# Gated scan and mixture of experts: softmax sums travel with the rows, running offsets are copied sooner, two selections go to GpSimd, and one unit's transposes move ahead of its rank matmuls

## The chip, the cores and the metric

One core of a Trainium2 chip runs the whole program. The metric is the device time of one execution in microseconds, shown as the median of several runs. A core has TensorE (PE; its loading of weights is PEld), VectorE (DVE), ScalarE (ACT), GpSimd (POOL) and SyncE (SP), each with its own queue, and 16 DMA engines that all queues share.

## The reference

```python
# x, f_logit: [4, 3648, 256]; lower_bound: [256]; all float32
sig = 1 / (1 + exp(-f_logit))
f = lower_bound + (1 - lower_bound) * sig
for t in range(3648):                       # per sequence
    h = f[:, t] * h + (1 - f[:, t]) * x[:, t];  y[:, t] = h
x = y.reshape(14592, 256)
g_logits = x @ w_group                      # [N, 4]
g_idx = argmax(g_logits);  g_sm = exp(g_logits - max)
g_w = (g_sm / (sum(g_sm) + 1e-9))[g_idx]
for g in range(4):                          # rows with g_idx == g
    e_logits = xg @ w_expert[g]             # [., 4]; e_idx, e_w in the same way
    for e in range(4):                      # rows with e_idx == e
        h = relu(xg @ w1[g, e])             # [., 1024]
        out[tok] = g_w * e_w * (h @ w2[g, e])
```

Sixteen experts, 14592 tokens of 256 values, a hidden width of 1024. Since the chosen logit is the greatest, its exponential is 1, and the weight of a row is one over the product of two softmax sums.

## The kernel before, in words

**Phase 1** goes through the tokens in 29 units of 512 (`UNIT`; the last has 256), with the 256 channels in two halves on the partitions. Per unit: load x and the gate logits (`p1_load`), tanh and an affine pass on ScalarE (`p1_tanh`, `p1_affine`), the gate's product and two scans on VectorE (`p1_tb`, `p1_gate`, lines 250, 261, 271), router logits on TensorE (`p1_router`, `p1_logits`, lines 308, 321), and `p1_back`, which transposes h on TensorE (line 289) and copies it with ScalarE into `rows` (line 291), a tile of 512 rows by `RW` = 258 words: 256 values, the token's number (line 293) and its weight.

**Routing** works on a group of units (`GROUPS`: eight single units, ten pairs, a last single one); `route_thunks` cuts it into steps. `s1` and `s2` find maxima and the one-hot of the winner on VectorE, `f3` the one-hot over 16 experts, `f4` the rank matmuls on TensorE (lines 423 to 426), which add up ranks and the running offsets of the 16 lists, `f4x` the exponentials on ScalarE, `s6` the sums (four VectorE operations, lines 367 to 374), `f5` the position of each row (lines 437, 439) and the copy of the new running offset to SBUF (`runoff`, line 441, ScalarE), `s8` the reciprocal into the last column of `rows` (line 380), `s7` the scatters: one indirect DMA by GpSimd for 128 rows into the list of their expert, `xs` (line 398). Later groups use `s3`, `s4`, `s5` instead of `f3`, `f4`, `f5`. `choose` and `place` read the running offset: `choose` picks the fullest lists that were not yet picked, `place` says which rows of a list may be read already.

**Phase 2** multiplies. Sixteen early jobs of kind A take 256 to 640 rows of a picked list each as soon as phase 1 has passed a cut (`EARLY`), while phase 1 goes on; sixteen late jobs of kind B take what is left, in an order that `order` computes when all is routed. Rows come back from `xs` by `job_rows`; the weight and the number travel with them, in `xr` and `meta` for A, in `info` and `joint` for B. `job_xt` transposes and splits a float32 number into two 16-bit parts, `job_split` does so for weights (lines 995, 997), `m1_step` multiplies by w1, takes the relu on ScalarE and the rest of the split on VectorE (lines 1133 to 1139), `m2_step` multiplies by w2 (line 1165), scales with ScalarE by the row's weight (line 1177) and scatters to the output (line 1179). The first four jobs (`RAW`) use float32 throughout (lines 1102, 1146). A chunk's `m2_step` calls come behind the `m1_step` calls of the chunk that follows, in the first four jobs right behind its own.

**Order.** `p1_thunks` lists phase 1 as small steps; `bg_step` mixes them into the jobs at a rate that due times set. `back(u - 1)` in that list puts the transposes of a unit in two steps; for units from 6 on they stand in front of `s1` already, before that behind `f4`. The start, until unit 5's routing, is in order as written for PE, DVE and ACT; later on a planner orders these engines within the limits that the program sets. SP's queue is in the order of the program.

Of the kernel before, what the change touches and what calls it, by code (L numbers as in the profile page):

```python
# [56 lines left out]
def gated_scan_moe(ctx: ExitStack, tc, zx, lower, wroute, wexp, out, S):  # L57
# [12 lines left out]
    RW = D + 2  # L70
# [70 lines left out]
    dmat = iota_f32("dmat", [P], [[1, P]], mult=-1)  # L141
# [186 lines left out]
    def route_thunks(G, T, fast=False):  # L328
# [3 lines left out]
        def s1():  # L332
# [3 lines left out]
            ge = R["ge"] = rt.tile([P, T, 5, 4], F32, name="ge")  # L336
            V.tensor_tensor(out=ge, in0=lg, in1=mx[:, :, :, None].broadcast_to([P, T, 5, 4]), op=ALU.subtract)

        def s2():
# [4 lines left out]
            oh = R["oh"] = rt.tile([P, T, 5, 4], F32, name="oh")  # L344
# [563 lines left out]
    def job_rows(j):  # L908
# [528 lines left out]
```

## Time and profile before

| | us |
|---|---|
| median of 3 runs | 746.05 (746.03 to 747.53) |
| profiled execution | 747.26 |
| its span, first to last instruction | 745.2 |
| TensorE busy | 707.5 (95%) |
| VectorE busy | 513.8 (69%) |
| ScalarE busy | 444.9 (60%) |
| GpSimd busy | 302.6 (41%) |
| mean granted clock of TensorE | 0.992 of full speed |

The profile is of one execution. Busy time counts an engine's own instructions; a matmul's end is modelled. In a timeline, a bracket behind an instruction holds how long its engine idled in front of it and what released it. Lines are those of the program printed above. The chain that ended last lies for 63% of the span on TensorE and for 13% on VectorE.

### The profile page before, as it was taken

How to read it: one execution, taken by the hardware profiler on the slowest of the kernel's cores; microseconds unless marked ns; L12 is line 12 of the kernel's file. 1: busy time of each engine (PE TensorE's matmuls, PEld its weight loads, DVE VectorE, ACT ScalarE, POOL GpSimd, SP SyncE). 2: the span in 40 equal slices, each digit the busy share in tenths (PEclk: the TensorE clock that was granted, in tenths of full speed). 3: DMA queues.
4: the chain of work that ended last, by engine and by line, in shares of the span. 5: the costliest groups of instructions: out<-in, count | busy, mean ns of one | idle time of the engine just before them, and what ended most of it. 6: DMA issues, size and time to landing. Idle time of an engine off the chain costs nothing.

```text
span 745.2 us, 18005 instructions
## 1 busy us (share of the span) xinstructions
PE 707.5 (95%) x6539; PEld 582.4 (78%) x6543; DVE 513.8 (69%) x1084; ACT 444.9 (60%) x824; POOL 302.6 (41%) x330
## 2 busy tenths in 40 slices
PE   2669999999999999999999999999999999999996
PEld 1457888888888888889989676877698888767795
DVE  6989658899999966595655755467336665676630
ACT  6667767986787864554555644566346555565531
POOL 3767367668877864632212111221131311212222
PEclk9989999999999999999999999999999999999998
DMA  8988799989999872747993281753362674666100
GB/s 326 414 293 280 238 371 288 413 295 315 322 327 288 242 233 71 221 108 199 209 223 111 91 188 38 180 154 117 114 163 99 193 193 150 181 186 189 41 30 31
DMA packets 99787, 151.36 MB, mean 203 GB/s; under 512 B 59593, under 2 KB 69594, under 8 KB 96880
## 3 DMA queue, kind: packets, MB, share of 16 engines
q1 hardware_dynamic: 85408, 102.83, 47.4%
q0 software_dynamic: 11168, 30.02, 10.8%
q10 hardware_dynamic: 3120, 17.34, 6.7%
q8 instruction: 52, 0.85, 0.5%
q14 instruction: 39, 0.32, 0.1%
HBM read 112.48 MB, written 37.93 MB: 202 GB/s over the span
## 4 chain that ended last, share of the span: by engine, by line
PE 63%; DVE 13%; issue 12%; DMA 4%; ACT 3%; POOL 3%; SPq 1%; POOLq 0%; DVEq 0%; ACTq 0%
PE ps_m L1165 25%; PE ps_m L1133 6%; PE ps_m L1135 6%; PE ps_m L1134 6%; PE ps_m L1146 4%; PE ps_m L1102 4%; DVE h L261 3%; POOL out_dram L1179 3%; PE ps_p L1135 3%; PE ps_p L1133 2%; PE ps_p L289 2%; PE ps_p L1134 2%; DVE w L997 2%; DMA xs<-rows,posi 2%; DVE hl L1139 2%
## 5 line engine op out<-in xcount | busy, mean ns | idle before, releaser
L1165 PE MATMUL ps_m<-w,hh 128*128 128x256 f16 (+4 forms) x1140 | 208.9, 272 | 0.0
L1165 PE MATMUL ps_m<-w,hl 128*128 128x256 f16 (+4 forms) x676 | 180.0, 271 | 0.0
L997 DVE TENSOR_TENSOR w<-st,w 128x1024 bf16<-128x1024 f32 x112 | 135.6, 1219 | 53.5 <-ACT w L995 52.0
L398 POOL DMA_INDIRECT xs<-rows,posi x114 | 136.5, 1198 | 73.8 <-ACT rows L293 20.7
L1179 POOL DMA_INDIRECT out_dram<-o,info x61 | 64.2, 1053 | 234.3 <-ACT o L1177 198.9
L1165 PE MATMUL ps_m<-w,rows 128*128 128x256 f16 (+4 forms) x848 | 128.4, 267 | 0.0
L995 ACT CAST w<-st 128x1024 f16<-128x1024 f32 x112 | 116.0, 1045 | 15.6 <-PE ps_m L1165 11.2
L1133 PE MATMUL ps_m<-xh,w 128*128 128x256 f16 (+9 forms) x494 | 120.4, 257 | 2.4 <-DVE hl L1139 2.4
L1165 PEld LDWEIGHTS <-hh 128*128 128x128 f16 (+5 forms) x1140 | 111.3, 100 | 12.4
L1135 PE MATMUL ps_m<-xh,w 128*128 128x256 f16 (+9 forms) x494 | 120.3, 257 | 0.0
L1134 PE MATMUL ps_m<-xl,w 128*128 128x256 bf16 (+9 forms) x494 | 120.3, 257 | 0.0
L1139 DVE SCALAR_TENSOR_TENSOR hl<-ps_m,hh 128x512 bf16<-128x512 f32 (+7 forms) x107 | 71.5, 672 | 45.5 <-ACT hh L1138 45.5
L1134 PEld LDWEIGHTS <-w 128*128 128x128 f16 x800 | 78.2, 98 | 24.8 <-issue 3.0
L1133 PEld LDWEIGHTS <-w 128*128 128x128 f16 x800 | 78.2, 98 | 23.4 <-issue 1.8
L1179 POOL DMA_INDIRECT out_dram<-o,meta x47 | 54.3, 1155 | 103.6 <-ACT o L1177 82.2
L1135 PEld LDWEIGHTS <-w 128*128 128x128 bf16 x800 | 78.1, 98 | 22.7 <-issue 0.2
L1165 PEld LDWEIGHTS <-rows 128*128 128x128 f16 (+3 forms) x848 | 77.9, 100 | 10.0 <-issue 0.6
L1138 ACT ACTIVATE hh<-ps_m 128x512 f16<-128x512 f32 (+7 forms) x107 | 63.3, 592 | 34.6 <-PE ps_m L1135 33.4
L1177 ACT ACTIVATE o<-ps_m,info 128x256 f32<-128x256 f32 (+6 forms) x61 | 28.5, 468 | 82.2 <-PE ps_m L1165 65.3
L1165 PEld LDWEIGHTS <-hl 128*128 128x128 bf16 (+4 forms) x676 | 66.2, 100 | 6.9
L261 DVE TENSOR_TENSOR_SCAN h<-zt,h 128x512 f32<-128x512 f32 (+3 forms) x48 | 56.8, 1194 | 2.0 <-PE ps_p L289 1.5
L1138 ACT ACTIVATE rows<-ps_p 128x512 f16<-128x512 f32 (+7 forms) x60 | 31.0, 516 | 24.8 <-PE ps_p L1135 24.7
(209 smaller groups left out, 1211.6 us busy)
## 6 DMA issues: line engine op xcount, KB each, us to landing
st<-in_wexp_dram SPq DMA_DIRECT2D x112, 512.0 KB
zt<-in_zx_dram ACTq DMA_DIRECT2D x16, 1024.0 KB
w<-in_wexp_dram SPq DMA_DIRECT2D x16, 512.0 KB
xs<-blank SPq DMA_DIRECT2D x26, 258.0 KB
zt<-in_zx_dram SPq DMA_DIRECT2D x6, 1024.0 KB
st<-in_zx_dram SPq DMA_DIRECT2D x8, 512.0 KB
xr<-xs SPq DMA_DIRECT2D x12, 258.0 KB
xr<-xs SPq DMA_DIRECT2D x16, 129.0 KB
```

Source lines behind the costliest of these rows:

```text
L261: sn = nc.vector.tensor_tensor_scan(out=h[:, k, c0 - a:c1 - a], data0=ff[:, k, c0 - a:c1 - a], data1=uu[:, k, c0 - a:c1 - a], initial=init ...
L398: sc = nc.gpsimd.indirect_dma_start(out=xs_v[G["t0"] + t][:, :], out_offset=bass.IndirectOffsetOnAxis(ap=R["posi"][:, t:t + 1], axis=0), i ...
L995: nc.scalar.copy(j.wh[i], j.st[i])
L997: nc.vector.tensor_tensor(out=j.wl[i], in0=j.st[i], in1=j.wh[i], op=ALU.subtract)
L1102: nc.tensor.matmul(pm[:, n * w:(n + 1) * w], (j.wh, j.wl)[c // 4][k][:, c % 4 * P:(c % 4 + 1) * P], x[:, 0:w], start=(k == 0), stop=(k == ...
L1133: nc.tensor.matmul(po, w1_at(j.wh, k, c), xh[:, k], start=(k == 0), stop=False)
L1134: nc.tensor.matmul(po, w1_at(j.wh, k, c), xl[:, k], start=False, stop=False)
L1135: nc.tensor.matmul(po, w1_at(j.wl, k, c), xh[:, k], start=False, stop=(k == KD - 1))
L1138: eviction[0] = nc.scalar.activation(hi, pv, AF.Relu).ins
L1139: nc.vector.scalar_tensor_tensor(out=h_at(j.hl[ch], cs, slice(0, w)), in0=pv, scalar=0.0, in1=hi, op0=ALU.max, op1=ALU.subtract)
L1165: nc.tensor.matmul(pm[i * q:i * q + n, 0:dw], h_at(h[ch], [c], ts)[:, 0], w2_at(w, c)[:, i * dw:(i + 1) * dw], start=(c == 0 and s == 0), ...
L1179: nc.gpsimd.indirect_dma_start(out=out_v[out_n[0]].rearrange("n (g d) -> (n g) d", g=g), out_offset=bass.IndirectOffsetOnAxis(ap=lt[s, r, ...
```

## The change

Five things are done. (1) A row has 262 words instead of 258: `s6` writes the five sums, four of them masked by the winning group, straight into `rows`, two VectorE operations for each unit of a group, and `s8` with the reciprocal is gone. The product and the reciprocal are made by `shares`, three VectorE operations, called behind the last `m1_step` of a chunk (kind A) or of a job's first chunk (kind B), and the scaling reads its result `wt`. All that carries the metadata is six words wide instead of two. (2) The copy of the running offset is a step of its own, `f5r`; in units up to `FAST` it stands in front of `back`. (3) Where `choose` picks two jobs with different cuts, their selections run on GpSimd. (4) `back` of unit 3 stands in front of `s1`. (5) `ge` and `oh` have one buffer, and `dmat` borrows the tile `rs`.

```diff
-    RW = D + 2
+    RW = D + 6
+    nc.gpsimd.memset(blank.bitcast(F32)[:, D + 1:RW], 1.0)
-    dmat = iota_f32("dmat", [P], [[1, P]], mult=-1)
+    dmat = p1.tile([P, P], F32, name="rs")
+    nc.gpsimd.iota(dmat, pattern=[[1, P]], base=0, channel_multiplier=-1, ...)
...
         def s6():
-            sm = rt.tile([P, T, 5], F32, name="sm", bufs=1)
-            V.tensor_reduce(out=sm, in_=R["ex"], axis=AX, op=ALU.add)
-            se = rt.tile([P, T, 4], F32, name="se", bufs=1)
-            V.scalar_tensor_tensor(out=se, in0=sm[:, :, 1:5], scalar=1e-9, in1=R["oh"][:, :, 0, :],
-                                   op0=ALU.add, op1=ALU.mult)
-            s1_ = rt.tile([P, T], F32, name="s1")
-            V.tensor_reduce(out=s1_, in_=se, axis=AX, op=ALU.add)
-            s2_ = rt.tile([P, T], F32, name="s2")
-            V.scalar_tensor_tensor(out=s2_, in0=sm[:, :, 0], scalar=1e-9, in1=s1_, op0=ALU.add, op1=ALU.mult)
-            R["s2"] = s2_
-
-        def s8():
             at = 0
             for rows, n in G["rows"]:
-                V.reciprocal(rows[:, 0:n, D + 1], R["s2"][:, at:at + n])
+                sm = rows[:, 0:n, D + 1:RW]
+                V.tensor_reduce(out=sm, in_=R["ex"][:, at:at + n], axis=AX, op=ALU.add)
+                V.scalar_tensor_tensor(out=sm[:, :, 1:5], in0=sm[:, :, 1:5], scalar=1e-9, in1=R["oh"][:, at:at + n, 0, :],
+                                       op0=ALU.add, op1=ALU.mult)
                 at += n
...
             placed[G["t0"]] = V.tensor_reduce(out=posi, in_=sc, axis=AX, op=ALU.add).ins
+            if not R.get("run"):
+                f5r()
+
+        def f5r():
+            pv = R["pp"][:, 0:(T + 1) * NE].rearrange("p (t e) -> p t e", e=NE)
             new = state["runoff"] = rt.tile([P, NE], F32, name="runoff")
             nc.scalar.copy(new, pv[:, T])
+            R["run"] = True
...
                     put(lambda u=u: p1_tanh(u + 1))
+                    if u == EARLY[0][0]:
+                        back(u - 1)
                     put(s1)
...
                     put(lambda u=u: p1_affine(u + 1))
+                    put(f5.soon)
                     back(u - 1)
...
+        B = nc.gpsimd if u >= BOOK else V
...
-                V.tensor_scalar(out=one, in0=key, scalar1=top[:, k:k + 1], scalar2=None, op0=ALU.is_equal)
+                B.tensor_scalar(out=one, in0=key, scalar1=top[:, k:k + 1], scalar2=None, op0=ALU.is_equal)
...
+    def shares(meta, n):
+        v = meta.bitcast(F32)
+        both = mo.tile([P, MT + 1], F32, name="both", bufs=2)
+        nc.vector.tensor_reduce(out=both[:, 0:n], in_=v[:, 0:n, 2:6], axis=AX, op=ALU.add)
+        nc.vector.scalar_tensor_tensor(out=both[:, 0:n], in0=v[:, 0:n, 1], scalar=1e-9, in1=both[:, 0:n],
+                                       op0=ALU.add, op1=ALU.mult)
+        wt = mo.tile([P, MT + 1], F32, name="wt", bufs=6)
+        nc.vector.reciprocal(wt[:, 0:n], both[:, 0:n])
+        return wt
+
+    def job_shares(j, ch):
+        if j.kind == "B":
+            n = sum(len(p) for p in j.parts)
+            if ch == 0 and n:
+                j.wt[0] = shares(j.info, n)
+            if ch == 0 and j.idx in SECOND:
+                j.wt["joint"] = shares(j.joint, 1)
+            return
+        a, w = j.chunks[ch]
+        for pi, (b, n) in enumerate(j.pieces):
+            if a <= b < a + w:
+                j.wt[pi] = shares(j.meta[pi], n // P)
...
+        if cs[-1] == KF - 1:
+            job_shares(j, ch)
...
-        nc.scalar.activation(o[s, 0:dw], pm[s, 0:dw], AF.Copy, scale=lt.bitcast(F32)[s, r, 1:2])
+        nc.scalar.activation(o[s, 0:dw], pm[s, 0:dw], AF.Copy, scale=wt[s, r:r + 1])
```

## Rows read from the trace of the kernel before

**Rows 1.** Windows: stretch, length, busy us by engine (instructions), clock, DMA share, GB/s
```profile
0.00:60.40 60.40, 34.06 (x276) 25.23 (x277) 49.20 (x152) 39.66 (x82) 36.66 (x66) 0.94 0.92 350
60.40:132.70 72.30, 72.30 (x500) 60.70 (x500) 53.15 (x123) 50.73 (x110) 44.63 (x56) 1.00 0.86 291
132.70:255.50 122.80, 119.79 (x1249) 104.28 (x1248) 121.51 (x243) 101.61 (x192) 92.58 (x86) 1.00 0.93 315
255.50:745.20 489.70, 481.32 (x4517) 392.19 (x4520) 289.91 (x568) 252.89 (x444) 128.74 (x125) 1.00 0.52 144
```

**Rows 2.** Timeline of TensorE: start, length, line, tiles, in brackets the idle before
```profile
51.65 0.21 PE L424 MATMUL ps_p<-oh16f,upto 128*128 128x64 bf16 x1 [3.19 <-DVE oh16f L412]
...
60.38 0.19 PE L424 MATMUL ps_p<-oh16f,upto 128*128 128x64 bf16 x1 [0.75 <-DVE oh16f L412]
...
159.48 0.27 PE L1133 MATMUL ps_m<-xh,w 128*128 128x256 f16 x1 [1.09 <-DVE hl L1139]
...
256.20 0.27 PE L1133 MATMUL ps_m<-xh,w 128*128 128x256 f16 x1 [0.99 <-DVE hl L1139]
...
328.58 0.27 PE L1133 MATMUL ps_m<-xh,w 128*128 128x256 f16 x1 [0.33 <-DVE hl L1139]
```

**Rows 3.** Timeline of VectorE, the end of unit 2's routing
```profile
28.70 0.17 DVE L369 SCALAR_TENSOR_TENSOR se<-sm,oh 128x16 f32<-128x16 f32 x1
28.91 0.17 DVE L372 TENSOR_REDUCE s<-se 128x4 f32<-128x16 f32 x1
...
29.20 0.22 DVE L437 TENSOR_TENSOR sc<-ps_p,oh16f 128x64 f32<-128x64 f32 x1
...
29.59 0.17 DVE L380 RECIPROCAL rows<-s 128x4 f32<-128x4 f32 x1
29.67 1.25 DVE L261 TENSOR_TENSOR_SCAN h<-zt,h 128x512 f32<-128x512 f32 x1
```

**Rows 4.** Timeline of TensorE, rank matmuls and transposes of units 2 and 3
```profile
28.60 0.32 PE L426 MATMUL ps_p<-oh16f,ones 128*128 128x64 bf16 x4
28.77 1.95 PE L289 MATMUL ps_p<-ident,h 128*128 128x128 f32 x8
...
36.17 0.21 PE L424 MATMUL ps_p<-oh16f,upto 128*128 128x64 bf16 x1 [2.83 <-DVE oh16f L412]
```

**Rows 5.** Timeline of ScalarE, units 2 and 3
```profile
27.71 1.50 ACT L234 ACTIVATE st<-st,mid,half 128x512 f32<-128x512 f32 x2
...
30.75 0.59 ACT L291 COPY rows<-ps_p 128x512 f32<-128x512 f32 x1 [0.17 <-PE ps_p L289]
31.24 0.18 ACT L441 COPY runoff<-ps_p 128x16 f32<-128x16 f32 x1
...
35.12 0.27 ACT L432 ACTIVATE ex<-ge 128x80 f32<-128x80 f32 x1 [1.21 <-DVE ge L337]
```

**Rows 6.** Timeline of VectorE, readers of the running offset, and two selections
```profile
31.52 0.18 DVE L660 SCALAR_TENSOR_TENSOR fill<-runoff,least 128x16 f32<-128x16 f32 x1 [0.59 <-ACT runoff L441]
...
39.04 0.18 DVE L706 SCALAR_TENSOR_TENSOR posA<-runoff,taken 128x16 int32<-128x16 f32 x1 [0.53 <-ACT runoff L441]
...
39.93 0.35 DVE L674 TENSOR_SCALAR sel<-fill,top 128x16 f32<-128x16 f32 x2
```

**Rows 7.** Timeline of GpSimd: a selection, first scatters of units 3 and 4
```profile
37.52 1.01 POOL L683 TENSOR_TENSOR least<-least,gone 128x16 f32<-128x16 f32 x1
38.69 1.05 POOL L398 DMA_INDIRECT xs<-rows,posi  x1 [0.16 <-DVE h L261]
...
46.46 1.05 POOL L398 DMA_INDIRECT xs<-rows,posi  x1 [1.60 <-ACT rows L293]
```

**Rows 8.** Timeline of SyncE's queue: the first expert rows
```profile
47.48 0.89 SPq L970 DMA_DIRECT2D xr<-xs  x2
```

**Rows 9.** VectorE by line and form, 132.7 to 255.5: count, busy us, mean ns, idle
```profile
L1139 DVE SCALAR_TENSOR_TENSOR hl<-ps_m,hh 128x512 bf16<-128x512 f32 x37 | 24.7, 677 | 0.2 <-ACT hh L1138 0.2
...
L367 DVE TENSOR_REDUCE sm<-ex 128x40 f32<-128x160 f32 x5 | 1.5, 308 | 0.0
```

More of the change, by code (lines that the diff above doesn't have):

```diff
@@ L140, in gated_scan_moe @@
     nc.gpsimd.memset(nowhere, N)
[L141 removed]
+    dmat = p1.tile([P, P], F32, name="rs")
+    nc.gpsimd.iota(dmat, pattern=[[1, P]], base=0, channel_multiplier=-1, allow_small_or_imprecise_dtypes=True)
     tri = const.tile([P, P], BF16, name="tri")
@@ L335, in s1 @@
             V.tensor_reduce(out=mx, in_=lg, axis=AX, op=ALU.max)
-            ge = R["ge"] = rt.tile([P, T, 5, 4], F32, name="ge")
+            ge = R["ge"] = rt.tile([P, T, 5, 4], F32, name="ge", bufs=1)
             V.tensor_tensor(out=ge, in0=lg, in1=mx[:, :, :, None].broadcast_to([P, T, 5, 4]), op=ALU.subtract)
@@ L343, in s2 @@
             V.tensor_reduce(out=pm, in_=pw, axis=AX, op=ALU.max)
-            oh = R["oh"] = rt.tile([P, T, 5, 4], F32, name="oh")
+            oh = R["oh"] = rt.tile([P, T, 5, 4], F32, name="oh", bufs=1)
             V.tensor_tensor(out=oh, in0=pw, in1=pm[:, :, :, None].broadcast_to([P, T, 5, 4]), op=ALU.is_equal)
@@ L447, in route_thunks @@
         if fast:
-            return s1, f4x, s2, f3, f4, s6, lambda: (f5(), s8()), s7s
-        return s1, s2, s3, s4, s5, lambda: (s6(), s8()), s7s
+            f5.soon = f5r
+            return s1, f4x, s2, f3, f4, s6, f5, s7s
+        return s1, s2, s3, s4, s5, s6, s7s
     def p1_thunks(us, groups, parts):
@@ L886, in make_job @@
         j.xh, j.xl = {}, {}
+        j.wt = {}
         return j
@@ L929, in job_rows @@
                     in_=xs[bass.ds(pos, j.blocks * 32), q * KD * 32:(q + 1) * KD * 32].rearrange("(i p) c -> p i c", p=32))
-            j.info = mo.tile([P, MT + 1, 2], I32, name="info", bufs=6)
+            j.info = mo.tile([P, MT + 1, RW - D], I32, name="info", bufs=6)
             if j.side:
@@ L933, in job_rows @@
                 if j.idx in PAIRS:
-                    joint[j.idx] = mo.tile([P, 2], I32, name="joint", bufs=2)
+                    joint[j.idx] = mo.tile([P, 1, RW - D], I32, name="joint", bufs=2)
                 j.joint = joint[SECOND.get(j.idx, j.idx)]
-                sync.dma_start(out=j.joint[at:at + n], in_=xs[bass.ds(pos + b, n), D:D + 2])
+                sync.dma_start(out=j.joint[at:at + n, 0], in_=xs[bass.ds(pos + b, n), D:RW])
             full = [p for ps_ in j.parts for p in ps_ if p[2] == 1]
@@ L963, in job_rows @@
                         early_loads.append(ld.ins)
-                    meta = mo.tile([P, 2, 2], I32, name="meta", bufs=16)
+                    meta = mo.tile([P, 2, RW - D], I32, name="meta", bufs=16)
                     ld = queue.dma_start(out=meta[:, 0:m],
-                                         in_=xs[bass.ds(at, w), D:D + 2].rearrange("(t p) c -> p t c", p=P))
+                                         in_=xs[bass.ds(at, w), D:RW].rearrange("(t p) c -> p t c", p=P))
                     early_loads.append(ld.ins)
@@ L1025, in job_xt @@
                                             scalar2=float(at - b), op0=ALU.subtract, op1=ALU.is_ge)
-                    nc.vector.copy_predicated(out=j.joint[s, 0:1], mask=gone[s], data=nowhere[s, 0:1])
+                    nc.vector.copy_predicated(out=j.joint[s, 0, 0:1], mask=gone[s], data=nowhere[s, 0:1])
                 if nf:
@@ L1075, in job_xt @@
         if j.raw:
-            j.meta.append(r[:, 0:m, D:D + 2])
+            j.meta.append(r[:, 0:m, D:RW])
             return
-        meta = mo.tile([P, 2, 2], I32, name="meta", bufs=16)
-        tc.keep_in_program_order(nc.vector.tensor_copy(meta[:, 0:m], r[:, 0:m, D:D + 2]))
+        meta = mo.tile([P, 2, RW - D], I32, name="meta", bufs=16)
+        tc.keep_in_program_order(nc.vector.tensor_copy(meta[:, 0:m], r[:, 0:m, D:RW]))
         if j.kind != "A":
@@ L1140, in m1_step @@
                                        op0=ALU.max, op1=ALU.subtract)
+        if cs[-1] == KF - 1:
+            job_shares(j, ch)
     def raw2(j, ch, t, cs, pm):
@@ L1169, in m2_step @@
         if j.kind == "B":
-            lt, r = j.info, b // P
+            lt, wt, r = j.info, j.wt[0], b // P
             if g > 1:
@@ L1203, in m2_joint @@
         o = mo.tile([P, D], F32, name="o", bufs=O_BUFS)
-        nc.scalar.activation(o, pm[:, 0:D], AF.Copy, scale=b.joint.bitcast(F32)[:, 1:2])
-        nc.gpsimd.indirect_dma_start(out=out_v[out_n[0]], out_offset=bass.IndirectOffsetOnAxis(ap=b.joint[:, 0:1], axis=0),
+        nc.scalar.activation(o, pm[:, 0:D], AF.Copy, scale=b.wt["joint"][:, 0:1])
+        nc.gpsimd.indirect_dma_start(out=out_v[out_n[0]], out_offset=bass.IndirectOffsetOnAxis(ap=b.joint[:, 0, 0:1], axis=0),
                                      in_=o, in_offset=None, bounds_check=N - 1, oob_is_err=False)
```

7 lines of the change are left out of this document (3 added, 4 removed).

## Prediction

> **What bounds the kernel now.** I read the windows first, cut where the limit changes [rows 1]. Up to 60.4 us TensorE works 34.06 of 60.40 us, so 26.3 of its 37.7 idle us lie in the start. From 60.4 to 132.7 it is busy 72.30 of 72.30: nothing but its own work counts. From 132.7 to 255.5 VectorE is busy 121.51 of 122.80 us and TensorE 119.79: two engines at their limit, and the 3.0 us that TensorE loses are there. Behind 255.5 TensorE is busy 481.32 of 489.70 us, most of the rest being the last eviction and scatter, and VectorE only 289.91.
>
> The timeline of TensorE says who holds it [rows 2]. The rank matmuls of units 5 and 6 (51.65, 60.38) wait 3.19 and 0.75 us for VectorE's one-hot. Later it has three waits of about 1 us, the first 1.09 at 159.48, the last 0.99 at 256.20, all for VectorE, and one of 0.33 at 328.58. So the sum has two sides: what VectorE saves ahead of 60 us moves everything forward, and what it is given between 132.7 and 255.5 comes back as stalls.
>
> **The change, part by part.**
>
> *Softmax sums, at the start.* Today, behind the gate's product (28.70), two more small operations follow at a pitch of 0.21 (28.70 to 28.91, operations that depend on each other), then the position product at 29.20, the reciprocal at 29.59, the next scan at 29.67, 0.08 behind it (operations that don't depend) [rows 3]. Without the two, the position product could start at 28.70 + 0.08 = 28.78, but its input, the rank matmuls, ends at 28.60 + 0.32 = 28.92 [rows 4]; I take 28.97. That gains 0.23, and the reciprocal's 0.08 goes too: 0.31 a unit. Five units (0 to 4) stand ahead of the rank matmuls of unit 5, in a row in which VectorE hardly waits: 1.55 us. Bounds: 5 x 0.08 = 0.4 (only the reciprocal) and 5 x 0.58 = 2.9 (two dependent steps and two independent ones).
>
> *Offsets copied sooner.* The copy of the running offset runs at 31.24, behind two copies of rows (the second 30.75, 0.59 long) [rows 5], and VectorE waits 0.59 us for it at 31.52 and 0.53 at 39.04 [rows 6]. Behind the affine pass it can start at 27.71 + 1.50 = 29.21, where the rank matmuls are done (28.92) [rows 4, 5]; VectorE asks only after its scan (29.67 + about 1.25). Both waits go: 1.12 us. What is late next there is nothing on the list; VectorE goes straight on to the gate. Behind the copy on ScalarE stand the row copies, held by their transposes anyway; cost 0, and 0.18 a unit without that cover. From unit 10 on the copy stays where it was.
>
> *Selections.* Two on VectorE at 39.93 took 0.35, some 0.26 of the chain [rows 6]. On GpSimd they stand in front of unit 4's scatters, where it idles 1.60 us until 46.46 [rows 7]. Gain 0.26; cost 0, and at worst 2 x 1.01 (the longest small GpSimd operation, at 37.52, ran 1.01 [rows 7]) less the 1.60, so 0.4 on a scatter.
>
> *Transposes of unit 3 ahead of its rank matmuls.* Eight take 1.95 us (28.77) and fall into a gap of 2.83 us in front of 36.17 [rows 4]. ScalarE's two copies of 0.59 and a short one go ahead of the exponential at 35.12, in front of which it idles 1.21 [rows 5]: it may come 0.2 late, and the sum that needs it stands five operations further on. Value 0; from -0.5 (if unit 3's scatters start sooner after all) to +0.2. No DMA is issued in another order; its scatters gain little: GpSimd is busy with the selection until 37.52 + 1.01 = 38.53 and begins unit 3 at 38.69 [rows 7].
>
> Sum to 51.65: 1.55 + 1.12 + 0.26 = 2.9. From 51.65 to 60.38 TensorE idles only the 0.75 [rows 2], and unit 5 gives VectorE its saving of 0.31 and a shorter wait there, so I add 0.7: **3.6 us gained at 60.4**, bounds 1.5 and 4.9. The first expert's rows are no brake: their load is issued at 47.48 [rows 8], and the transposes need it behind the rank matmuls and eight transposes, at 51.65 - 2.9 + 1.95 = 50.7.
>
> *Shares downstream, 60.4 to 132.7.* Four jobs add three small VectorE operations each; VectorE has 72.30 - 53.15 = 19 us free [rows 1]. Cost 0, at most 4 x 0.51 = 2.0 without that.
>
> *Shares downstream, 132.7 to 255.5.* In this stretch 37 evictions of 512 columns run on VectorE [rows 9]; at four for a chunk of 256 rows and two for one of 128, that is six jobs with ten chunks (4+4, 6+6, 8+8 evictions; the 37th begins the next). So ten calls, thirty operations of about 0.17 (reciprocal 29.59, reduction 28.91 [rows 3]). One call costs 3 x 0.09 = 0.27 if other work stands between its steps, and 0.21 + 0.21 + 0.09 = 0.51 if not; I take 0.39, the middle, since the order of VectorE here is a planner's and both kinds of neighbour occur: 3.9 us. Five routing groups go from six operations to four [rows 9]; the wide reduction of 0.31 becomes two of 0.23, so that a group saves 0.2 at the shorter pitch and nothing at the longer: 1.0 us. VectorE has 1.29 us unused [rows 1]; I let 0.6 soak up. The bill: 3.9 - 1.0 - 0.6 = **2.3 us**, bounds 0.4 (2.7 - 1.0 - 1.3) and 5.1 (ten by 0.51). As VectorE's queue is full from end to end, it reaches TensorE at 256.20 whole.
>
> In the rows dependent neighbours follow at 0.21 and independent ones at 0.08, though one takes 0.17 [rows 3]. The Trainium skill, "VectorE: DVE Perf Modes", Rules for kernel authors, tells instead to minimize the count of operations, because a drain follows each whatever it depends on. By it the net twenty operations cost 20 x 0.17 = 3.4 us (an estimate) and the sum becomes -3.6 + 3.4 - 0.6 + 0.4 = -0.4; the trace agrees with it for dependent neighbours only.
>
> *Behind 255.5.* Each of the 16 late jobs and three joint tiles gets a call (19 x 0.51 = 9.7 us if it were all on the path), but VectorE has 200 us free there and the tile that reads the share is evicted a chunk later: 0. At 328.58, where VectorE is late already by 0.33 [rows 2], one call more in front costs 0.4 (bounds 0 and 0.5). Rows longer by 16 of 1032 bytes: 1.6% on scatters and row loads, up to 60.4 us beside DMA engines at 0.92, on no wait above; 0, at most 0.3. Smaller buffers for routing tiles make VectorE wait for VectorE only: 0.
>
> **Sum.** -3.6 + 2.3 + 0.4 = -0.9 us. On the profiled execution (747.26, span 745.20 and 2.06 around it) that gives 746.4; the median shown is 746.05, 1.21 lower, so the prediction is 746.05 - 0.9 = 745.15, own range 743.8 to 746.5 (a bill of 0.9 to 3.7).
>
> **Rivals.**
> 1. *The bill is hidden.* Planned anew, the calls lie where VectorE would wait, or where its lateness doesn't reach TensorE. For: in 122.80 us of full VectorE TensorE has only three long waits [rows 2], so there is play between the two. Against: VectorE has 1.29 us unused in 122.80. Bill 0.4, no late stall: -3.2, 742.85.
> 2. *The bill outgrows the gain.* One mechanism: the three steps of a call stand next to each other behind the last eviction of a chunk, 0.51 each, nothing is saved in the groups, none soaks up, and the start gives only 2.9 (unit 6 still waits): -2.9 + 5.1 + 0.4 = +2.6, 748.65. It decides from a bill above the gain of the start, so above 0.3 us a call when the start gives 2.9. For: dependent steps at full pitch in [rows 3]. Against: in the full stretch there is always other work to stand between.
> 3. *The start is held by the first rows, not by VectorE.* GpSimd's scatters are back to back (38.53, 38.69) and move only by three units' saving, 3 x 0.31 = 0.9, and if loading the rows takes over, the gain is 0.9: -0.9 + 2.3 + 0.4 = +1.8, 747.85. Against: 47.48 is 3.2 us ahead of the need.
> 4. *Every operation costs its full length.* VectorE's 20 net operations by 0.17, less 0.6 of unused time: -0.4, 745.65. Against: the pitch of 0.08 [rows 3]. (This is the count rule of the Trainium skill, "VectorE: DVE Perf Modes", named above.)
>
> **Chances.** Forecast 0.45, hidden bill 0.22, outgrown 0.18, first rows 0.08, full length 0.07. About 0.2% (1.5 us: 744.55 and 747.55) is what a measurement of this kernel tells from no change. A third of the forecast's chance lies under 744.55, with rival 1 that gives faster 0.37; slower 0.26 (rivals 2 and 3); same 0.37. The range reaches from the hidden bill, 742.6, to the outgrown one, 748.6.
>
> **What would show it.** Unit 5's rank matmuls at 48.8 instead of 51.65, unit 6's at 56.8 instead of 60.38, no wait of VectorE for the offset behind units 2 and 3. The stretch of full VectorE then starts near 129, and the stalls of TensorE in it grow from 3.0 to some 5 us, the last ending near 255. Wrong, if the rank matmuls of unit 6 move by under 2 us, if TensorE's idle time in that stretch doesn't grow, or if a new wait stands in the late jobs, such as an eviction waiting for its share.

## The result: slower, 757.46 against 746.35 us

The median went from 746.35 us (4 runs, 746.03 to 747.53) to 757.46 us (4 runs, 756.32 to 758.31): ratio 1.0147, interval 1.0129 to 1.0166. The forecast was 745.15 with a range to 748.6, so the sign and the size were wrong. The profiled execution took 756.32 us (747.26 before), its span 754.3 (745.2); TensorE was busy 710.8 us (707.5), VectorE 521.1 (513.8), ScalarE 444.7 (444.9), GpSimd 307.5 (302.6).

### The profile after

Lines of the changed kernel have other numbers: the scan is L263 (L261 before), the gate L252 and L273 (L250, L271), the rank matmuls L416 to L419 (L423 to L426), the one-hot oh16f L405 (L412), product and positions L430 and L432 (L437, L439), the copy of the running offset L439 (L441), the scatter L391 (L398), m1's split L1168 (L1139). New are L371 and L372 (the sums) and L1101, L1102, L1105 (a call of `shares`).

The windows of the kernel after answer to [rows 1]; each cut lies at the work at which before was cut, moved by the shift of the nearest TensorE instruction that both have. The last two windows are the wait that the text comes to, and the time behind it.

```profile
0.00:59.15 59.15, 34.44 (x275) 24.97 (x276) 47.16 (x135) 38.73 (x81) 38.12 (x65) 0.80 0.91 346
59.15:139.80 80.65, 74.62 (x498) 61.33 (x498) 52.94 (x123) 50.66 (x109) 48.70 (x59) 0.96 0.81 268
139.80:264.43 124.63, 120.48 (x1251) 104.95 (x1250) 122.95 (x264) 102.46 (x193) 89.73 (x85) 1.00 0.92 314
264.43:754.30 489.87, 481.30 (x4517) 392.77 (x4520) 298.03 (x665) 252.88 (x444) 130.91 (x126) 1.00 0.52 144
86.97:91.45 4.48, 0.00 (x0) 0.02 (x1) 3.80 (x12) 0.81 (x2) 0.00 (x0) 0.63 0.30 74
91.45:109.64 18.19, 18.19 (x117) 15.06 (x117) 11.99 (x26) 10.20 (x23) 9.36 (x13) 0.90 0.88 292
```

The start became 1.25 us shorter, the second stretch 8.35 longer, though before TensorE was busy there in 72.30 of 72.30 us; the third grew by 1.83, the last by 0.17. So nearly all of the loss lies where the forecast had put a cost of 0.

The timeline of TensorE after names it; its first two lines and its last answer to [rows 2]:

```profile
50.98 0.21 PE L417 MATMUL ps_p<-oh16f,upto 128*128 128x64 bf16 x1 [2.90 <-DVE oh16f L405]
...
59.15 0.19 PE L417 MATMUL ps_p<-oh16f,upto 128*128 128x64 bf16 x1 [0.20 <-DVE oh16f L405]
...
91.45 0.26 PE L417 MATMUL ps_p<-oh16f,upto 128*128 128x128 bf16 x1 [4.49 <-DVE oh16f L405]
...
265.13 0.27 PE L1162 MATMUL ps_m<-xh,w 128*128 128x256 f16 x1 [1.05 <-DVE hl L1168]
```

The wait of 4.49 us is new. Before, the same matmul, that of the pair of units 8 and 9, waited for nothing (its timeline of TensorE):

```profile
87.42 0.23 PE L424 MATMUL ps_p<-oh16f,upto 128*128 128x128 bf16 x1
```

The new wait ends with a one-hot of VectorE, as the waits of the start do, but VectorE was not busy with it. The timeline of VectorE after: units 2 to 4 and 7 (these answer to [rows 3, 6]), then what came ahead of that one-hot:

```profile
29.42 0.22 DVE L430 TENSOR_TENSOR sc<-ps_p,oh16f 128x64 f32<-128x64 f32 x1 [0.39 <-ACT runoff L439]
...
36.75 0.22 DVE L430 TENSOR_TENSOR sc<-ps_p,oh16f 128x64 f32<-128x64 f32 x1 [0.83 <-ACT runoff L439]
...
45.78 1.20 DVE L273 SCALAR_TENSOR_TENSOR st<-st 128x1024 f32<-128x1024 f32 x1
47.02 1.33 DVE L263 TENSOR_TENSOR_SCAN h<-st,h 128x512 f32<-128x512 f32 x1
...
48.40 1.27 DVE L263 TENSOR_TENSOR_SCAN h<-st,h 128x512 f32<-128x512 f32 x1
...
67.60 0.22 DVE L430 TENSOR_TENSOR sc<-ps_p,oh16f 128x64 f32<-128x64 f32 x1 [1.24 <-ACT runoff L439]
...
85.51 0.16 DVE L1101 TENSOR_REDUCE both<-xr 128x2 f32<-128x8 f32 x1 [9.42 <-DMA xr<-xs]
...
85.99 2.44 DVE L263 TENSOR_TENSOR_SCAN h<-zt,h 128x512 f32<-128x512 f32 x2
88.87 0.16 DVE L1101 TENSOR_REDUCE both<-xr 128x2 f32<-128x8 f32 x1 [0.44 <-DMA xr<-xs]
...
91.11 0.29 DVE L405 TENSOR_TENSOR oh16f<-oh 128x128 bf16<-128x128 f32 x1
```

Two things are to be seen. At 85.51 the first operation of a call of `shares`, 0.16 us long, stands 9.42 us at the head of VectorE's queue, because its rows `xr` are still on their way (SyncE's queue issues their load at 82.84). The two scans, the maxima and the one-hot of units 8 and 9 stand behind it. In the timeline of VectorE before, the same scans and maxima wait too, but for work of TensorE and ScalarE, and come earlier:

```profile
78.09 2.52 DVE L261 TENSOR_TENSOR_SCAN h<-zt,h 128x512 f32<-128x512 f32 x2 [1.54 <-PE ps_p L289]
...
83.11 0.32 DVE L335 TENSOR_REDUCE mx<-Lg 128x40 f32<-128x160 f32 x1 [2.50 <-ACT Lg L322]
```

And at 29.42, 36.75 and 67.60 the product waits for the copy of the running offset (L439): the wait that was to go has changed sides.

ScalarE after, to be held against [rows 5]: the copy does start as the affine pass ends, as forecast (29.21). But the product, which did not wait before [rows 3], now waits until the copy is done.

```profile
27.83 1.50 ACT L236 ACTIVATE st<-st,mid,half 128x512 f32<-128x512 f32 x2
29.24 0.15 ACT L439 COPY runoff<-ps_p 128x16 f32<-128x16 f32 x1
```

GpSimd after, to be held against [rows 7]. The selections of unit 4 run from 44.64 to 49.68 (48.48 + 1.20) and hold its first scatter, which comes at 49.84 instead of 46.46:

```profile
36.98 0.22 POOL L686 TENSOR_TENSOR least<-least,gone 128x16 f32<-128x16 f32 x1
...
44.64 2.44 POOL L682 TENSOR_SCALAR sel<-fill,top 128x16 f32<-128x16 f32 x1
...
47.25 1.15 POOL L685 TENSOR_SCALAR gone<-sel 128x16 f32<-128x16 f32 x1
48.48 1.20 POOL L686 TENSOR_TENSOR least<-least,gone 128x16 f32<-128x16 f32 x1
49.84 1.06 POOL L391 DMA_INDIRECT xs<-rows,posi  x1 [0.16 <-DVE ge L339]
```

SyncE's queue after: the first expert rows are issued as early as in [rows 8].

```profile
47.38 0.89 SPq L974 DMA_DIRECT2D xr<-xs  x2
```

VectorE by line and form after, from 143.0 to 264.8, to be held against [rows 9]: again 37 evictions, and now nine share reductions of this form (two more are of one column; the forecast had ten calls).

```profile
L1168 DVE SCALAR_TENSOR_TENSOR hl<-ps_m,hh 128x512 bf16<-128x512 f32 x37 | 24.7, 675 | 0.0
...
L1101 DVE TENSOR_REDUCE both<-meta 128x2 f32<-128x8 f32 x9 | 1.2, 148 | 0.0
```

Where time is lost or won is seen best at marks that all kernels have. This table gives the start of the same TensorE instruction in the profile of each: the rank matmuls of unit 5, unit 6, units 8 and 9, units 10 and 11, two of the matmuls that read the tile `scn` of the later routing, the matmul of [rows 2] that waits about 1 us near 256, and the last matmul. Below the first line stand differences from it. A mark has noise: kernels that are alike up to unit 6 differ there by 0.4 us (e18 and before) and by 0.5 to 0.6 (e16 and e17). And each row is one execution: that of e12 (750.09) is 2.1 us above its median, that of e13 (748.79) 1.2 below.

```
                        unit 5  unit 6    8-9  10-11    scn    scn   256.2    last
before                   51.65   60.38  87.42 103.96 126.08 150.91  256.20  737.79
after                    -0.67   -1.23  +4.03  +5.68  +5.67  +7.86   +8.93   +8.99
e1  shares behind        -0.77   -0.86  +0.10  +0.09  +0.66  +3.40   +4.67   +4.72
e16 and copy late        -1.87   -1.89  -1.53  -1.54  -1.24  +0.20   +0.97   +1.03
e17 and later blanks     -1.37   -1.28  -0.91  -0.92  -0.92  -0.91   +0.22   +0.28
e12 as e16, sel. on DVE  -1.64   -2.50  -1.56  -1.56  -0.88  +2.24   +3.00   +3.06
e10 copy sooner alone    +0.02   +0.05  +0.46  +0.45  +0.86  +4.07   +4.03   +4.04
e13 product, copy sooner +1.72   +1.37  +1.61  +1.65  +1.65  +1.65   +1.40   +1.40
```

### The profile page after: what moved, and what is told of

Read it like the earlier page. It is cut to its first block, busy times and chain, and to the rows that moved or that the text cites. A ratio compares the mean times of both kernels' runs of the same rounds, so it can differ in the third digit from the quotient of the medians.

```text
span 754.3 us, 18084 instructions
## 1 busy us (share of the span) xinstructions
PE 710.8 (94%) x6539; PEld 584.0 (77%) x6543; DVE 521.1 (69%) x1185; ACT 444.7 (59%) x824; POOL 307.5 (41%) x333
## 4 chain that ended last, share of the span: by engine, by line
PE 59%; issue 11%; DMA 11%; DVE 9%; ACT 4%; POOL 4%; SPq 1%; POOLq 0%; DVEq 0%; ACTq 0%
PE ps_m L1196 25%; PE ps_m L1162 6%; PE ps_m L1164 6%; PE ps_m L1163 6%; POOL out_dram L1210 3%; PE ps_p L1164 3%; PE ps_p L1162 3%; DMA st<-in_wexp_dram 3%; PE ps_p L1163 3%; DVE h L263 2%; DMA xs<-rows,posi 2%; DMA zt<-in_zx_dram 2%; PE ps_m L1129 2%; DMA xs<-blank 2%; DMA xr<-xs 2%
## 5 line engine op out<-in xcount | busy, mean ns | idle before, releaser
L391 POOL DMA_INDIRECT xs<-rows,posi x114 | 135.5, 1189 | 91.2 <-issue 18.6
L1208 ACT ACTIVATE o<-ps_m,wt 128x256 f32<-128x256 f32 (+6 forms) x116 | 54.7, 473 | 129.4 <-PE ps_m L1196 102.7
L1168 DVE SCALAR_TENSOR_TENSOR hl<-ps_m,hh 128x512 bf16<-128x512 f32 (+7 forms) x107 | 71.4, 670 | 38.5 <-ACT hh L1167 38.3
L1210 POOL DMA_INDIRECT out_dram<-o,meta x47 | 51.8, 1103 | 103.4 <-ACT o L1208 73.6
L263 DVE TENSOR_TENSOR_SCAN h<-zt,h 128x512 f32<-128x512 f32 (+3 forms) x48 | 56.6, 1192 | 0.6
```

Source lines behind the costliest of these rows:

```text
L263: sn = nc.vector.tensor_tensor_scan(out=h[:, k, c0 - a:c1 - a], data0=ff[:, k, c0 - a:c1 - a], data1=uu[:, k, c0 - a:c1 - a], initial=init ...
L391: sc = nc.gpsimd.indirect_dma_start(out=xs_v[G["t0"] + t][:, :], out_offset=bass.IndirectOffsetOnAxis(ap=R["posi"][:, t:t + 1], axis=0), i ...
L1168: nc.vector.scalar_tensor_tensor(out=h_at(j.hl[ch], cs, slice(0, w)), in0=pv, scalar=0.0, in1=hi, op0=ALU.max, op1=ALU.subtract)
L1208: nc.scalar.activation(o[s, 0:dw], pm[s, 0:dw], AF.Copy, scale=wt[s, r:r + 1])
L1210: nc.gpsimd.indirect_dma_start(out=out_v[out_n[0]].rearrange("n (g d) -> (n g) d", g=g), out_offset=bass.IndirectOffsetOnAxis(ap=lt[s, r, ...
```

## The experiments

Each kernel was timed over five rounds against the kernel before on the same chip; a ratio is to that one. On the chip of the runs e5 to e8 the kernel before itself took 758.49 us, its engines idling at times with no releaser in the profile, so these four were run again on another chip as e9 to e12, and those values count.

**The shares held back (e1).** The calls of the first four jobs are tied behind the job's last eviction of the first layer, so that they can't stand in front of a scan while their rows are under way.

```diff
-    def shares(meta, n):
+    def shares(meta, n, behind=None):
...
-        nc.vector.tensor_reduce(out=both[:, 0:n], in_=v[:, 0:n, 2:6], axis=AX, op=ALU.add)
+        rd = nc.vector.tensor_reduce(out=both[:, 0:n], in_=v[:, 0:n, 2:6], axis=AX, op=ALU.add)
+        if behind is not None:
+            tc.add_manual_dep(rd.ins, behind.name, ...)
...
-                j.wt[pi] = shares(j.meta[pi], n // P)
+                j.wt[pi] = shares(j.meta[pi], n // P, j.ev)
```

> The change, with the shares of the four raw jobs tied behind the job's last first-layer eviction; nothing else is altered. Theory A (the shares of raw jobs stand in VectorE's queue ahead of scans and one-hots and wait there for rows that have not landed): the wait of 9.42 us at 85.51 goes, TensorE's 4.49 us at 91.45 goes with it, and the time falls by 6 to 9 us, to 748 to 751. Theory B (the sum of the added small operations and the longer rows is what costs): the same operations still run, so 755 to 758. Theory C (the start is what failed: the position product waits for the offset's copy): the start is unchanged here, so 755 to 758.

Measured 752.21 us, ratio 1.0070 (1.0057 to 1.0083). In the timeline of TensorE of this kernel the wait is gone:

```profile
87.52 0.23 PE L417 MATMUL ps_p<-oh16f,upto 128*128 128x128 bf16 x1
```

That is 87.42 before and 91.45 after. Half of the loss, 0.77% or 5.7 us, is the place of these small calls in VectorE's queue. Both waits went as theory A said, but the time fell by less than its 6 to 9 us: 0.7% is left.

**Copy at its old place (e2), transposes at theirs (e3), the other parts without the sums (e4).**

```diff
                     put(lambda u=u: p1_affine(u + 1))
-                    put(f5.soon)                        # e2
...
-                    if u == EARLY[0][0]:                # e3
-                        back(u - 1)
```

For e4 the kernel before got the sooner copy, the moved transposes and the selections on GpSimd, but kept its sums and its reciprocal, and has no `shares`.

> The change without the sooner offset copy: it is issued behind the positions again. Theory A (queue held by the shares): the wait for the rows stays, 754 to 758, though the rank matmuls of unit 5 come earlier than 50.98, at 50.0 to 50.5, because the position product no longer waits for ScalarE (0.39, 0.83 and 0.52 us in three units), while VectorE waits for the copy behind the scan again. Theory C (the position product's new wait is the cause): 750 to 753.

> The change with unit 3's transposes behind its rank matmuls again. Theory A: 755 to 759, unit 4's and 5's rank matmuls within 0.5 us of 43.26 and 50.98. Theory D (the transposes in front of the rank matmuls take TensorE's clock and delay the rest: granted clock 0.51 and 0.50 in 30 to 50 us against 1.00 and 0.83 before): 751 to 754 with the clock of 30 to 50 back above 0.8.

> The kernel before with the other three parts (offset copy sooner, selections on GpSimd, unit 3's transposes first), so without the scattered sums: six routing operations a group, a reciprocal, no shares in the jobs, rows of 258 words. Theory A: no share, so no wait for rows in VectorE's queue, and within 1.5 us of before (745 to 748); the position product still waits for the offset's copy, so the rank matmuls of unit 5 gain at most 0.5 of 51.65. Theories C and D (copy or transposes are the cause): 751 to 757.

Measured: e2 754.61 us, 1.0098 (1.0083 to 1.0112); e3 757.61, 1.0148 (1.0135 to 1.0161); e4 752.08, 1.0061 (1.0049 to 1.0074). The transposes are worth nothing either way. The sooner copy costs: without it the change is 0.5% less slow (e2), and e4, which has no new VectorE operation at all, is slower by as much as e1, where theory A had expected no loss. Their profiles differ, though: in that of e4 TensorE itself waits 2.24 us for rows `xr` at 76.95 and is 3.43 us late at units 8 and 9, so e4 alone doesn't say which part costs.

**One part alone, and the shares held back without the others (e5 to e12).** On the kernel before: the selections on GpSimd (e5, e9), the sooner copy (e8, e10). On e1: the selections back on VectorE (e6, e11), then the copy late too (e7, e12).

```diff
+        B = nc.gpsimd if u >= BOOK else V               # e5, e9; e6, e11 undo it
-                V.tensor_scalar(out=one, in0=key, ...)
+                B.tensor_scalar(out=one, in0=key, ...)
...
+                    put(f5.soon)                        # e8, e10; e7, e12 undo it
```

> The kernel before with the two selections of a cut on GpSimd and nothing else. Theory G (GpSimd is the brake: a small GpSimd operation that meets a long one of VectorE's ends only with it, as 37.52 least 1.01 ended with VectorE's scan at 38.5; two more of them put unit 4's first scatter near 48.5 instead of 46.46, the scatters run back to back from there, and the row loads of the next jobs come 1 to 3 us later): 749 to 752, with the row load of 80.13 at 82 or later. Theory C (the offset's copy is what cost 5 us in the runs that keep it): within 1 us of before, 746 to 748.

> The change with the raw jobs' shares behind the first layer (as in the run that gave 752.21) and also the selections on VectorE again. Theory G: another 2 to 5 us less, 747 to 750, unit 4's first scatter at 46.5 or sooner. Theory C: no change from 752.21, within 1 us.

> The change with the shares behind the first layer, the selections on VectorE, and the offset's copy behind the positions again; what is left is the scattered sums and unit 3's transposes. Theory G: 746 to 749, no different from the version that keeps the copy by more than 1 us. Theory C: 746 to 748 while the version that keeps the copy stays above 751. Both expect the rank matmuls of unit 5 at 50.2 or sooner, since the position product no longer waits for ScalarE.

> The kernel before with the sooner offset copy and nothing else. The position product waits for ScalarE's copy (0.4 to 0.8 us a unit, as in the changed kernel), so the rank matmuls of unit 5 stand at 51.3 to 52.5 and gain nothing. Theory G: 745.5 to 748. Theory C: 750 to 753.

> The kernel before with the two selections on GpSimd alone, taken again: in the first run of it the engines stood idle up to 20 us with nothing that released them (TensorE 5.8, VectorE 19.9 us before 340 us; before: 0.0 and 0.7), and so did the kernel before, at 758.49. Theory G (GpSimd's longer stretch delays scatters, row loads and then everything): 749 to 752. Theory C (the sooner copy is the cause of the 5 us that the three other parts cost): within 1 us of before.

> The kernel before with the sooner offset copy alone, taken again for the same reason. Theory C: 749 to 753, TensorE's new waits of 0.7 and 1 to 2 us near 130 and 135 (for ScalarE) show up here as in every run that keeps the copy. Theory G: 745.5 to 748.

> The change with the shares behind the first layer and the selections on VectorE, taken again. Theory G: 747 to 749.5 (against 752.21 with the selections on GpSimd). Theory C: 751 to 753, the loss between 126 and 157 us still there (3 us longer than before's 29.6 us between the two scans of those stretches).

> The same with the copy behind the positions too, so only the scattered sums and unit 3's transposes are left of the change. Theory C: 745 to 748, and 3 to 6 us below the version that keeps the copy. Theory G: within 1 us of the version that keeps it.

```
                                  first chip                 second chip
selections alone      e5  758.08  0.9996 (0.9977-1.0016)   e9  747.36  1.0007 (0.9998-1.0016)
shares behind, sel.   e6  769.97  1.0161 (1.0125-1.0197)   e11 751.54  1.0056 (1.0044-1.0068)
 and copy late        e7  765.05  1.0083 (1.0054-1.0113)   e12 748.00  1.0023 (1.0004-1.0043)
copy sooner alone     e8  765.57  1.0088 (1.0055-1.0121)   e10 751.30  1.0053 (1.0040-1.0066)
```

The selections make no difference, so theory G (GpSimd is the brake) fails in e9 and e11. Moving one ScalarE copy of 0.16 us forward costs 0.53%, 4.0 us, by itself, and e11 loses most of its excess when the copy goes back (e12). How it does that can be followed in the timelines of e10 (VectorE, ScalarE, GpSimd, SyncE's queue, again ScalarE and its queue, TensorE):

```profile
62.38 1.23 DVE L271 SCALAR_TENSOR_TENSOR zt<-zt 128x1024 f32<-128x1024 f32 x1 [0.34 <-ACT zt L234]
63.52 0.22 DVE L437 TENSOR_TENSOR sc<-ps_p,oh16f 128x64 f32<-128x64 f32 x1
...
64.85 0.20 DVE L439 TENSOR_REDUCE posi<-sc 128x4 int32<-128x64 f32 x1
...
60.84 1.51 ACT L234 ACTIVATE zt<-zt,mid,half 128x512 f32<-128x512 f32 x2
62.25 0.16 ACT L446 COPY runoff<-ps_p 128x16 f32<-128x16 f32 x1
...
65.82 1.42 POOL L398 DMA_INDIRECT xs<-rows,posi  x1 [4.29 <-ACT rows L291]
...
83.00 2.91 SPq L979 DMA_DIRECT2D xr<-xs  x4
...
122.87 1.54 SPq L706 DMA_DIRECT2D xs<-blank  x2
124.61 5.65 SPq L996 DMA_DIRECT2D st<-in_wexp_dram  x5
...
125.68 1.04 ACT L1004 CAST w<-st 128x1024 f16<-128x1024 f32 x1 [2.25 <-DMA st<-in_wexp_dram]
...
132.77 0.34 ACTq L210 DMA_DIRECT2D zt<-in_zx_dram  x1
133.16 0.60 ACT L1114 ACTIVATE hl<-ps_m 128x512 f32<-128x512 f32 x1 [4.80 <-DMA xs<-blank]
...
133.81 1.13 PE L1155 MATMUL ps_m<-w,hl 128*128 128x256 f32 x4 [1.61 <-ACT hl L1114]
```

and in those of before, the same places:

```profile
60.70 0.23 DVE L437 TENSOR_TENSOR sc<-ps_p,oh16f 128x64 f32<-128x64 f32 x1 [0.37 <-PE ps_p L426]
60.96 0.22 DVE L439 TENSOR_REDUCE posi<-sc 128x4 int32<-128x64 f32 x1
...
62.92 1.27 POOL L398 DMA_INDIRECT xs<-rows,posi  x1 [1.90 <-ACT rows L293]
...
80.13 3.33 SPq L970 DMA_DIRECT2D xr<-xs  x4
...
120.23 1.49 SPq L697 DMA_DIRECT2D xs<-blank  x2
121.93 3.42 SPq L987 DMA_DIRECT2D st<-in_wexp_dram  x4
...
121.93 1.99 ACT L995 CAST w<-st 128x1024 f16<-128x1024 f32 x2
...
124.61 0.33 ACTq L210 DMA_DIRECT2D zt<-in_zx_dram  x1
```

Product (VectorE) and copy (ScalarE) read the same tile in PSUM, `ps_p`, one behind the other in the order of the program; that the product waits for the copy is in the rows; that it is the shared tile that orders them is read from the program, not tested. Before, the copy followed the product; in e10 the product follows the copy, the copy the affine pass (60.84 to 62.35), and in the order of the planner the gate and then a scan stand ahead of product and positions. Positions come 3.9 us later, GpSimd's scatter 2.9, the load of the rows 2.9, the blank writes and the weight load 2.6 and 2.7. At 125.68 ScalarE stands 2.25 us for these weights; then it comes to a load of x at 132.77 (124.61 before) that by the profile waits for a blank write, and the relu behind it waits 4.80. This wait of the relu (4.07 to 5.03 us) stands in the profiles of all eight kernels that have the copy ahead of the product and this load in ScalarE's queue (after, e1, e3, e4, e6, e8, e10, e11) and in no other. Each held step is small; the order of the queues passes the delay on. How it is handed through each transfer is read from times, not tested: a load of rows between these two (113.95, before 112.71) is only 1.24 late.

**The order of product and copy repaired (e13, e14).** In e13, on the kernel before, product, positions and copy all go ahead of the transposes and row copies. In e14 the changed kernel has the shares held back and the same order; no wait for the copy is left.

```diff
                     put(lambda u=u: p1_affine(u + 1))   # e14; e13 likewise
-                    put(f5.soon)
+                    put(f5)
                     back(u - 1)
...
-                    put(f5)
```

> The kernel before with the position product, the positions and then the offset's copy all ahead of the transposes and row copies: the copy is as early as in the change, but the product is in front of it in the program. Theory P (the product's wait for the copy makes the positions of unit 6 late, and scatters, row loads and weight loads behind them): 745.5 to 747.5, unit 6's positions at 61.2 or sooner, no wait of VectorE for the copy ahead of the product, and no loss between 120 and 154 us. Rival Q (a copy in front of the row copies costs by itself, by the later row copies): 749 to 752, as with the copy alone (751.3).

> The change with the shares of raw jobs behind the first layer and the product ahead of the copy; all four parts are kept. Theory P: 746 to 749 (start gain of 1.6 to 3 us less the shares' bill of 1.9 us, and whatever of the start is lost where weights arrive no sooner). Rival Q: 751 to 753, as without this repair (751.54, 752.21).

Measured: e13 750.01 us, 1.0053 (1.0038 to 1.0068); e14 747.49, 1.0015 (1.0004 to 1.0026). So in the changed kernel the repair gives back what the copy cost (e1 has 1.0070). In e13 it doesn't: 750.01 is in the range of rival Q, not of theory P. In both profiles the loss between the two `scn` marks is gone: e13 takes 24.83 us and e14 25.13 (24.83 before, 28.04 in e10). In e13 the weight load that is issued at 121.93 before comes 1.51 us later (123.44), but TensorE is 1.65 late itself there, and no wait for it shows. Such a loss isn't the copy's alone: e16, without it, loses 1.44 there, and the execution of e12 that was profiled 3.12, at a granted clock of 0.94. But e13 pays at the start, since the sums no longer fill the time until the rank matmuls are done. Its timeline of VectorE, the product in units 2 and 4 (between them 0.44 in unit 3):

```profile
30.14 0.23 DVE L437 TENSOR_TENSOR sc<-ps_p,oh16f 128x64 f32<-128x64 f32 x1 [0.37 <-PE ps_p L426]
...
45.73 0.23 DVE L437 TENSOR_TENSOR sc<-ps_p,oh16f 128x64 f32<-128x64 f32 x1 [0.37 <-PE ps_p L426]
```

Its rank matmuls of unit 5 are 1.72 us late (53.37), and its last matmul 1.40. The rest of its 0.53% isn't in its profiled execution, the shortest of its six, and stays unexplained. On the kernel before, the old place of the copy is thus the better one; on the changed kernel the two places are alike (e14, and e16 below).

**The load of x elsewhere (e15).** On e10, the load that stood in ScalarE's queue at 132.77 goes into GpSimd's.

```diff
-    (nc.sync if u < ZX_SP else nc.scalar).dma_start(...)
+    (nc.sync if u < ZX_SP else nc.gpsimd if u == 18 else nc.scalar).dma_start(...)
```

> The kernel before with the sooner copy alone (751.3), with one load (the input of unit 18, the one that waited 4.80 us in ScalarE's queue) issued from GpSimd's queue. If that wait is what reaches TensorE (1.61 us at 133.81, and what follows): 749 to 750. If the late weight load alone would cost the same: 751 to 752. If GpSimd, which gets the issue instead, holds scatters by it: above 752.

Measured 751.10 us, 1.0063 (1.0049 to 1.0077): no gain in the median. Its profiled execution, 749.24, is shorter than the median, and there the stretch between the `scn` marks is 26.35 instead of 28.04 us, with a wait of ScalarE for weights, 4.49 us at 135.74, in place of the relu's. The median is where the expectation put late weights as the cause, but how much of the 4 us is this load and how much the weights stays open.

**Both repairs by taking the copy back (e16), and the weights ahead of the blank writes (e17, e18).** e16 is e1 without the sooner copy. In e17, on top of it, from unit 10 on blank writes stand six weight loads further back in SyncE's queue; e18 is the kernel before with that alone.

```diff
-        ready[0] = True
+        ready[0] = ready[0] or pptr[0] + (6 if u >= 10 else 0)
...
-        if ready[0]:
+        if ready[0] and pptr[0] >= ready[0]:
```

> The change with the shares behind the first layer and the copy behind the positions, selections left on GpSimd (the run with them on VectorE gave 748.0). Start gain at unit 5's rank matmuls 1.5 us or more, bill of the shares 1.9 us between 150 and 300 us. If the start gain reaches the end: 745.5 to 747. If it is lost at the weight loads (as in the run that gave 748.0, 33.45 us from 118.4 to 151.9 against 29.6): 747.5 to 749.

> The change with the shares behind the first layer and the copy behind the positions (747.5), and from unit 10 on the blank writes of a list six weight loads later in SyncE's queue. Theory W (the late weight load takes the start gain): the cast's wait of 2.14 us at 123.6 goes, the stretch between the two scans (118.4 to 149.8) is back at 29.6 us, and the time falls by 1.5 to 2 us, to 745.5 to 746. Rival (something else bounds there, or the later blanks hold the next rows): 747 to 749.

> The kernel before with the same later blank writes and nothing else. Its cast does not wait for weights at 121.9, so theory W expects no gain here: 746 to 747. If later blanks are a gain by themselves: below 745.5.

Measured: e16 747.50 us, 1.0012 (1.0003 to 1.0021); e17 747.59, 1.0018 (1.0007 to 1.0030); e18 746.28, 0.9996 (0.9986 to 1.0005). e16 is 1.24 us ahead of before at the first `scn` mark and 0.20 behind at the second: sooner work meets weights that come when they came. The timeline of e16, ScalarE and TensorE:

```profile
123.58 1.04 ACT L999 CAST w<-st 128x1024 f16<-128x1024 f32 x1 [2.14 <-DMA st<-in_wexp_dram]
...
126.30 0.33 PE L323 MATMUL ps_p<-ident,rs 128*128 128x128 f32 x1 [1.24 <-ACT rows L293]
```

In e17 the same cast waits for nothing, and the second mark is reached at 150.00, 0.91 us ahead of before. The timeline of its ScalarE:

```profile
121.02 1.99 ACT L999 CAST w<-st 128x1024 f16<-128x1024 f32 x2
```

From there to the last matmul it needs 588.07 us (738.07 - 150.00) instead of 586.88, nearly all of it the shares' bill (105.29 before and 106.42 up to the mark of 256.2), so the lead is gone again. Theory W's fall by 1.5 to 2 us did not come. No kernel here beats the one before.

## Why the prediction was wrong, step by step

**Shares downstream, 60.4 to 132.7: "Cost 0, at most 4 x 0.51 = 2.0". This step failed, and it is the largest.** Measured: 5.26 us between the marks of unit 6 and units 8 and 9 (-1.23 to +4.03), and 1.65 more up to units 10 and 11, in a stretch that takes 18.19 us at a granted clock of 0.90 instead of 16.54 at 1.00; e1 removes both. The 19 us that VectorE had free are a sum over the stretch. What counted is when the operation's data were there and what stood behind it in VectorE's queue: a reduction of 0.16 us waited 9.42 us with scans and a one-hot behind it that TensorE needed. The place of a call was left to the planner; the forecast should have asked where its `xr` lands.

**Offsets copied sooner: gain 1.12, "What is late next there is nothing on the list". This failed too.** Alone it gave 0.0 us at 51.65 (e10), and beside the sums it cost 1.10 (e1 against e16) and 1.83 (e11 against e12). To the end it cost some 4 us: 4.0 of the median alone, and 0.58% or 4.3 us, the start's 1.10 among them, between e1 and e16. The forecast looked only at who waits for the copy. It didn't list what else reads that PSUM tile, which is the position product; with the copy ahead of it, VectorE waits 0.39 to 1.24 us for ScalarE, and positions and scatters come later by it (2.9 us at unit 6's first scatter in e10). That the copy costs is shown; how the delay goes on to the weights and to the load of x is in part read from times.

**Softmax sums: 1.55 us at 51.65. Right**, 1.64 measured in e12 (50.01), and 1.37 to 1.87 in e2, e16 and e17, which have the selections on GpSimd besides. **Transposes: 0. Right** (e3 against after: 757.61 and 757.46).

**Selections: 0.26, and at worst 0.4 on a scatter.** In time nothing (e9, 1.0007). On the scatter the bound was too low: unit 4's first came at 48.28 in e9 and at 49.84 after instead of 46.46, without an effect on the end in e9.

**3.6 us at 60.4.** 1.23 after; without the sooner copy 1.28 in e17, 1.89 in e16, 2.50 in e12 (57.88). The forecast named a shift under 2 us as a sign against it, and so it was: the copy's gain of 1.12 is missing, and beside the sums its place costs.

**Shares, 132.7 to 255.5: 2.3, and 0.4 at 328.58. The path was right, the size was not.** From the scan at 149.56 to the one at 250.73 VectorE takes 101.17 us before, 0.69 to 1.16 more in the nine kernels with shares (after, e1, e2, e3, e11, e12, e14, e16, e17), and from 0.25 less to 0.16 more in those without (e4, e9, e10, e13, e15, e18). From 150.91 to 256.20 TensorE takes 105.29 us before and 0.76 to 1.27 more with shares. So what VectorE lost did reach TensorE, as forecast, but it is about half of 2.3; ahead of 150.91 e2 and e17 show nothing of it (24.84 us between the `scn` marks). Which term of 3.9 - 1.0 - 0.6 was off no run separates. The late wait cost nothing: from the mark of 256.2 to the last matmul 481.65 us after, 481.59 before. The count rule cited in the prediction (the Trainium skill, "VectorE: DVE Perf Modes", Rules for kernel authors) would put an estimated 3.4 us on VectorE; what was measured lies well below that.

**The sum.** From 1.0147 to 1.0070 the shares' place (0.77%), from there to 1.0012 the copy (0.58%); what is left, 0.12% or 0.9 us, is the change without these two. In e16's profile it is made up of 1.24 us won up to the first `scn` mark, 1.44 lost behind it, where the weights did not come sooner, and 0.77 of bill. "What VectorE saves ahead of 60 us moves everything forward" was thus a third, smaller error: in e16 it stops at weights that stand behind row loads and blank writes in SyncE's queue. In e17 that wait is gone and 0.91 us of the lead pass it, but the bill there, 1.13, is larger, and the median is no lower; so what the late weights cost the median isn't shown. None of the rivals had either of the two large mechanisms; rivals 2 and 3 had the sign, but by other ways.

## What to carry to other kernels

Before adding a small operation to an engine that an ordering program fills, ask when its inputs land and what will stand behind it; free time of the engine is no cover, and an explicit dependency can hold it back (here it gave back 5.7 of 11 us). Before moving a reader of a PSUM tile forward, list its other readers and see on which engine's queue they will now wait. A gain at the start can be lost where the DMA issues that follow don't move with it, and one profiled execution isn't the median: compare stretches over several kernels before a size is believed.

## What the runs showed of the hardware

Small GpSimd operations stretch when they meet VectorE's long ones, and end with them. After, the selection at 44.64 took 2.44 us beside a scan (44.59 + 1.27) and the gate behind it, and ended at 47.08, the gate (45.78 + 1.20) at 46.98; the one at 47.25 ended at 48.40, the scan (47.02 + 1.33) at 48.35; the one at 48.48 ended at 49.68, the next scan (48.40 + 1.27) at 49.67. The same kind of operation took 0.22 us at 36.98 with no long operation beside it. The 1.01 us from which the forecast took its bound [rows 7] was such a case: that operation ended at 38.53, VectorE's scan (37.26 + 1.25) at 38.51. The Trainium skill, "SBUF — State Buffer", Who interferes with whom, says that a VectorE instruction with two inputs in SBUF and a GpSimd instruction that reads SBUF exclude each other for a whole instruction; these rows agree, with ends 0.01 to 0.10 us apart.

The granted clock of TensorE fell in the 4.48 us without a matmul (0.63) and was 0.90 in the 18.19 us behind, so part of both was at the lower level, 1.2 GHz; the 1.65 us above go with it. A low clock in the windows 20 to 40 us (0.75 after, 1.00 in e3) went with no difference in time (medians 757.46 and 757.61 us).
